# Second-attention scores moved ahead of the loop, and x in the places of the weight halves, in a two-layer MoE kernel

## The chip, the cores and the metric

The kernel runs on one core of one Trainium2 chip. The metric is the device time of one execution in microseconds (us), as the median of several runs; lower is better.

## The reference, cut to what matters

x has 12480 tokens of 128 channels, `inducing` has 32 rows. All data is float32.

```python
def mab(q, kv):                                # scale = 1/sqrt(128)
    s = scale * (q @ kv.T);  s = s - s.max(-1)
    a = np.exp(s);  a /= a.sum(-1) + 1e-9
    return a @ kv
h = mab(inducing, x)                           # first attention: 32 x 128, needs all of x
x = mab(x, h)                                  # second attention: 12480 x 128
g = s * relu(x @ w_in)**2 + b;  x = g @ w_out  # 128 -> 2048 -> 128
u = x @ moe2_w_in                              # 128 -> 2048
g = where(u >= 1, u, where(u <= -1, 0, (u + 1)**2 / 4))
return g @ moe2_w_out                          # 2048 -> 128
```

## The kernel before, in words

The tokens are cut into 25 blocks of 512 (the last has 192). The program has four parts.

**Front.** x is loaded in seven groups of four blocks (`load_x`, L272; groups 0 to 6, the last of one block). Each block is transposed on PE and copied by ACT into its own tile `xT` (`transposes`, L287), which stays for the whole kernel. From `xT` come the first attention's scores (`scores`, L303: tile `psc`, maximum, exponential `e`) and from x as loaded the weighted sum (`weighted`, L347: `pe`, `eT`, `ph`). The tile of x as loaded, `xc`, has four buffers (`XB = 4`), so the load of group g waits for the weighted sum `ph` of group g - 4. `finish` (L543) joins the groups into `hT` (128 x 32, four copies side by side), the only input that the second attention needs beside `xT`. The weights arrive as 64-bit floats in pieces of 512 columns (16 pieces: four each of `in`, `out`, `in2`, `out2`) and are converted by `convert` (L418) on ACT and DVE. The second layer's weights, and later w_out, are kept as two rounded halves, `hi` and `lo` (tiles `wi2_hi`, `wi2_lo`, `wo2_hi`, `wo2_lo`, `wo_hi`, `wo_lo`, each 128 x 2048).

**Ramp.** From `hT` on, the first 18 steps of the first layer (`ramp_step`, L889; a step is 256 hidden columns of one block, eight steps to a block) run between the rest of the conversions (`c_sum`, L457, has three matmuls for each piece of `in2` and `out2`), the products `hw = h @ w_in` (`h_w`, L843) and the softmaxes of block 0 and of group 1 (blocks 1 to 4; `all_softs`, L912).

**Loop.** Step t runs, on PE in this order, `in1` of step t (L639, tile `h`), `out2` (L764), `in2` of step t - 18 (L725, tile `h`), and `out1` of step t - 2 (L700). `in2` and both `out` products take three matmuls for each product of rounded halves. The elementwise work between them lies on ACT (relu, square, `hi`), DVE (clip, `g`, `lo`) and POOL (`hi`, `lo` of the first layer).

**Tail.** The last 18 steps of the second layer run without the first.

The second attention works on groups of up to four blocks: sizes 1, 4, 4, 4, 4, 4, 3, 1 (groups 0 to 7). For a group, `soft_scores` (L577) multiplies `hT[:, :32]` with `xT` of each block, four matmuls that fill the four 32-row strips of one PSUM bank. `soft_turn` (L585) transposes that in 32 x 32 squares on DVE into the SBUF tile `se`. Then come maximum, subtraction, exponential, sum, division and DMAs into place. In the loop these steps are called at fixed distances ahead of the block that needs them (`SOFT`, L47): scores and turn 22 steps ahead, maximum 21, and so on. In a loop step the scores stand on PE between `in2` and `out1`, and take the bank pair with the tag `h1`, which has a single buffer and is the one that `in1` writes in each loop step:

```python
ps = (mbank if g == 1 else bank)(f"s2_{g}")     # soft_scores; bank: tag h1, bufs=1; mbank: tag h2, bufs=2
p = mbank(f"h1_{t}") if t < LAG and t % 2 else bank(f"h1_{t}")   # in1
```

In the ramp `in1` takes `h1` and `h2` by turns; `h2` also serves `h_w` and the conversions (`cw`).

**What sets the order.** Front, ramp and the first four loop steps are ordered by a planner (`Plan`, L113). The string `JOBS` names jobs (`c` convert a piece, `x` load a group, `t` transposes, `s` scores, `w` weighted sum, `f` finish, `z` first softmax, `h`, `b`, `p` split a piece of w_out, `a` ramp step, `o` softmax of group 1, `q` next block's attention). In its order each operation takes the first gap on its engine that fits its estimated duration; the program is then emitted in order of planned start. Engines run their instructions in that order. All loads are issued by one queue (SP), in the planned order. PE gaps of the plan are filled with idle matmuls (`on_idle`, L1012; `on_idle0`, L1016). The second layer's buffers open at `close` (L936), after all conversions and splits. The loop follows `ORDER` (L72).

Of the kernel before, what the change touches and what calls it, by code (L numbers as in the profile page):

```python
# [10 lines left out]
F32 = mybir.dt.float32  # L11
# [26 lines left out]
NPC = DFF // PC  # L38
XB = 4
RAWB = 5  # L40
# [14 lines left out]
SQB = {"DVE": 1.0, "Pool": 3.0}  # L55
EVAC = ("ACT",)

# [116 lines left out]
def moe_attn_kernel(ctx: ExitStack, tc: tile.TileContext, x, ind, w_in, w_out, s, b, w_in2, w_out2, out):  # L174
# [12 lines left out]
    wo_lo = kt([128, FC, C], "wo_lo", F32R)  # L187
    wi2_hi = kt([128, DFF], "wi2_hi", F32R)
    wi2_lo = kt([128, DFF], "wi2_lo", F32R)
    wo2_hi = kt([128, FC, C], "wo2_hi", F32R)  # L190
    wo2_lo = kt([128, FC, C], "wo2_lo", F32R)
    hT = kt([C, 4 * NM], "hT")
# [225 lines left out]
    def convert(n, at=0.0):  # L418
# [35 lines left out]
        def c_hi(eng):  # L454
            copy(eng, wparts[name][0][:, sl], T["cva", n].bitcast(F32))

        def c_sum():  # L457
            ps = T["cw", n] = mbank(f"cw{n}")[:, 0, :]
            nc.tensor.matmul(ps, ident, T["cva", n].bitcast(F32), start=True, stop=False)  # L459
            nc.tensor.matmul(ps, minus_r, wparts[name][0][:, sl], start=False, stop=False)  # L460
            nc.tensor.matmul(ps, ident_r, T["cvl", n], start=False, stop=True)

        def c_lo(eng):
            copy(eng, wparts[name][1][:, sl], T.pop(("cw", n)))

# [6 lines left out]
        if name in ("in", "out"):  # L472
            P["c_add", n] = P["c_end", n] = best(ENG["add"], c_add, t, bias=CB)
        else:
            hi = best(ENG["hi"], c_hi, a)
            t = took("h2", 1.33, c_sum, hi, t, P["hT"])
            P["c_end", n] = best(ENG["lo"], c_lo, t)
            left["h2"].append(P["c_end", n])

    def split_out(n):  # L480

        k = pieces[n][1]
        sl = slice(k * PC, (k + 1) * PC)
        hi, lo = (w[:, sl] for w in wparts["out"])
        t = best(ENG["hi"], lambda e: copy(e, hi, T["w", n]), P["c_add", n])
        P["c_split", n] = best(ENG["rest"], lambda e: engine[e].tensor_sub(lo, T["w", n], hi.bitcast(F32)), t, bias=CB)

# [89 lines left out]
    def soft_scores(g):  # L577
        nb = sizes[g]
        ps = (mbank if g == 1 else bank)(f"s2_{g}")
        for i in range(nb):  # L580
            bl = first[g] + i
            nc.tensor.matmul(ps[NM * i:NM * (i + 1), 0, :tb(bl)], hT[:, :NM], xT[bl], start=True, stop=True)
        sm[g, "s"] = ps

    def soft_turn(g):  # L585

        n, cols = NM * sizes[g], tb(first[g])
        e = sm[g, "e"] = pool["wk"].tile([128, NQ, NM], F32, tag="se", name=f"se{g}", bufs=1)[:n, :cols // NM]
        nc.vector.transpose(e.rearrange("p q j -> p (q j)"), sm.pop((g, "s"))[:n, 0, :cols])  # L589

# [99 lines left out]

    def outp(t, hi, lo, whi, wlo, p, js=range(GW)):
        p = p[:, :tb(t // SPB)]
        for j in js:
            f = fch(t, j)
            first, last = f == 0, f == FC - 1
            nc.tensor.matmul(p, whi[:, f, :], hi[:, j, :], start=first, stop=False)  # L696
            nc.tensor.matmul(p, whi[:, f, :], lo[:, j, :], start=False, stop=False)  # L697
            nc.tensor.matmul(p, wlo[:, f, :], hi[:, j, :], start=False, stop=last)  # L698

    def out1(t):  # L700
        outp(t, hi1.pop(t), lo1.pop(t), wo_hi, wo_lo, acc1(t // SPB))

# [22 lines left out]
    def in2(t, js=range(GW)):  # L725
        bl = t // SPB
        if js[0] == 0:
            h2[t] = bank(f"h2_{t}") if t in tail and (t - tail[0]) % 3 == 0 else mbank(f"h2_{t}")
        p = h2[t]
        for j in js:  # L730
            f = fch(t, j)
            fs = slice(f * 128, (f + 1) * 128)
            nc.tensor.matmul(p[:, j, :tb(bl)], wi2_hi[:, fs], y1h[bl], start=True, stop=False)  # L733
            nc.tensor.matmul(p[:, j, :tb(bl)], wi2_lo[:, fs], y1h[bl], start=False, stop=False)  # L734
            nc.tensor.matmul(p[:, j, :tb(bl)], wi2_hi[:, fs], y1l[bl], start=False, stop=True)  # L735

# [27 lines left out]
    def out2(t, js=range(GW)):  # L764
        outp(t, hi2[t], lo2[t], wo2_hi, wo2_lo, acc2(t // SPB), js)

    def store(bl):
# [4 lines left out]
        for r in range(C // NM):  # L772
# [4 lines left out]
    misc = {}  # L777
    softs = {"scores": soft_scores, "turn": soft_turn, "top": soft_top, "sub": soft_sub, "e": soft_e,
             "sum": soft_sum, "mul": soft_mul, "move": soft_move}

    def at(t, f, *args):
        on_dve = f in (soft_turn, soft_top, soft_sum, soft_q)
        misc.setdefault((t, on_dve), []).append(lambda: f(*args))
# [22 lines left out]
    def f_se():  # L806
        e = sm[0, "e"] = wtile([128, NQ, NM], "se", "se0")[:TP, :KB, :]
# [61 lines left out]
    def ramp_soft(f):  # L869
        g = 1  # L870
        do = lambda *a: softs[f](g, *a)
        if f == "scores":
            in_use["g1"] = took("h2", 0.9, do)
        elif f in ("turn", "top", "sum"):
            P[f + "1"] = in_use["g1"] = add("DVE" if f == "turn" else "DVE+", {"turn": 0.7, "top": 0.69, "sum": 1.0}[f], do, in_use["g1"])
# [33 lines left out]
    def first_job():  # L909
        P["ind"], P["s"], P["s"] = loads()  # L910

    def all_softs():  # L912
        for f in softs:
            ramp_soft(f)
            if f == "turn":
                left["h2"].append(P["turn1"])

# [4 lines left out]
    def load(g):  # L922
        load_x(g, P.get(("ph", g - XB)))

    def step(a):
# [3 lines left out]
           "f": lambda _: finish(), "z": lambda _: first_soft(), "c": conv, "h": h_w, "b": b_cols, "p": split_out,  # L929
           "a": step, "o": lambda _: all_softs(), "q": ramp_q}  # L930
    for j in JOBS.split():
# [8 lines left out]

    P["close"] = add("switch", 0.01, close, *[o for k, o in P.items() if k[0] in ("c_end", "c_split")], *[P["out1", a] for a in range(LAG)], P["bcol"])
    P["cx"] = P["close"]
# [208 lines left out]
```

## Time and profile before

| | us |
|---|---|
| median of 3 runs | 1028.97 (1028.88 to 1030.15) |
| the profiled execution, its own time | 1030.76 |
| its span | 1028.9 |
| hT there (end of the front) | 50.3 |
| first `in2` matmul (end of the ramp) | 113.2 |
| PE busy in the span | 996.1 (97%) |
| DVE, ACT, POOL busy | 817.2, 846.6, 752.5 |

The span runs from the first to the last instruction of the profiled execution. Matmuls are pipelined and their ends modelled, so a busy PE is not PE at its peak. A float32 matmul leaves two records, a rounded one (`fp32r`) one.

### The profile page before, as it was taken

How to read it: one execution, taken by the hardware profiler on the slowest of the kernel's cores; microseconds unless marked ns; L12 is line 12 of the kernel's file. 1: busy time of each engine (PE TensorE's matmuls, PEld its weight loads, DVE VectorE, ACT ScalarE, POOL GpSimd, SP SyncE). 2: the span in 40 equal slices, each digit the busy share in tenths (PEclk: the TensorE clock that was granted, in tenths of full speed). 3: DMA queues.
4: the chain of work that ended last, by engine and by line, in shares of the span. 5: the costliest groups of instructions: out<-in, count | busy, mean ns of one | idle time of the engine just before them, and what ended most of it. 6: DMA issues, size and time to landing. Idle time of an engine off the chain costs nothing.

```text
span 1028.9 us, 12530 instructions
## 1 busy us (share of the span) xinstructions
PE 996.1 (97%) x4512; PEld 773.2 (75%) x4512; DVE 817.2 (79%) x838; ACT 846.6 (82%) x919; POOL 752.5 (73%) x507
## 2 busy tenths in 40 slices
PE   6899899999999999999999999999999999999997
PEld 4654577888778888778888778888778878888776
DVE  6888678787788878788878788777787878878884
ACT  5677888888888888888888888888888888887764
POOL 0211578888788788788888788888888878886466
PEclk9999999999999999999999999999999999999999
DMA  8521001100002000002000002000001000000000
GB/s 304 192 64 60 0 1 31 31 1 11 11 1 52 11 1 11 10 1 52 11 1 11 11 1 52 11 1 11 11 1 41 11 1 11 15 1 11 11 11 15
DMA packets 65469, 28.11 MB, mean 27 GB/s; under 512 B 54016, under 2 KB 58368, under 8 KB 65408
## 3 DMA queue, kind: packets, MB, share of 16 engines
q1 hardware_dynamic: 65408, 27.33, 10.9%
q8 instruction: 35, 0.57, 0.2%
q14 instruction: 26, 0.21, 0.1%
HBM read 14.80 MB, written 6.39 MB: 21 GB/s over the span
## 4 chain that ended last, share of the span: by engine, by line
PE 84%; DVE 10%; ACT 2%; DMA 2%; issue 1%; POOL 1%; SPq 0%; DVEq 0%; ACTq 0%; POOLq 0%
PE y L697 15%; PE y L696 15%; PE y L698 15%; PE h L733 9%; PE h L735 8%; PE h L734 8%; PE h L644 8%; DVE cl L740 3%; PE y L708 2%; DVE lo L761 2%; DMA xc<-in_x_dram 2%; DVE mx L607 1%; POOL lo L761 1%; DVE h L751 1%; PE cw L459 1%
## 5 line engine op out<-in xcount | busy, mean ns | idle before, releaser
L674 POOL TENSOR_TENSOR lo<-g,hi 128x1024 fp32r<-128x1024 f32 (+1 forms) x182 | 427.0, 2346 | 15.2
L740 DVE TENSOR_SCALAR cl<-h 128x1024 f32<-128x1024 f32 (+2 forms) x202 | 239.1, 1186 | 154.6 <-PE h L735 154.6
L744 ACT ACTIVATE cl<-cl,mhalf 128x1024 f32<-128x1024 f32 (+2 forms) x202 | 226.7, 1124 | 105.7 <-DVE cl L740 103.2
L697 PE MATMUL y<-lo,wo_hi 128*128 128x512 f32 (+1 forms) x764 | 299.8, 392 | 1.3 <-POOL lo L761 1.3
L698 PE MATMUL y<-hi,wo_lo 128*128 128x512 f32 (+1 forms) x764 | 299.5, 392 | 0.0
L696 PE MATMUL y<-hi,wo_hi 128*128 128x512 f32 (+1 forms) x764 | 299.5, 392 | 0.0
L226 POOL TENSOR_SCALAR hi<-g 128x1024 fp32r<-128x1024 f32 (+1 forms) x182 | 186.8, 1027 | 140.8 <-PE y L698 120.2
L751 DVE SCALAR_TENSOR_TENSOR h<-h,cl 128x1024 f32<-128x1024 f32 x182 | 223.1, 1226 | 12.4 <-ACT cl L744 1.2
L761 DVE TENSOR_TENSOR lo<-h,hi 128x1024 fp32r<-128x1024 f32 x182 | 221.2, 1216 | 2.7 <-ACT hi L222 1.9
L664 ACT ACTIVATE g<-g 128x1024 f32<-128x1024 f32 (+1 forms) x199 | 206.4, 1038 | 5.3
L657 ACT ACTIVATE g<-h 128x1024 f32<-128x1024 f32 (+1 forms) x194 | 191.5, 987 | 11.2 <-PE h L644 9.7
L222 ACT CAST hi<-h 128x1024 fp32r<-128x1024 f32 x182 | 181.9, 999 | 15.9 <-DVE h L751 15.9
L696 PEld LDWEIGHTS y<-hi,wo_hi 128*128 128x128 f32 x764 | 143.8, 188 | 38.2 <-POOL lo L674 4.2
L697 PEld LDWEIGHTS y<-lo,wo_hi 128*128 128x128 f32 x764 | 143.8, 188 | 35.7 <-POOL lo L761 2.5
L698 PEld LDWEIGHTS y<-hi,wo_lo 128*128 128x128 f32 x764 | 143.5, 188 | 33.4
L733 PE MATMUL h<-y1h,wi_hi 128*128 128x512 f32 (+1 forms) x400 | 157.4, 394 | 10.6 <-DVE lo L761 10.1
L735 PE MATMUL h<-y1l,wi_hi 128*128 128x512 f32 (+1 forms) x400 | 156.3, 391 | 0.0
L734 PE MATMUL h<-y1h,wi_lo 128*128 128x512 f32 (+1 forms) x400 | 156.0, 390 | 0.0
L644 PE MATMUL h<-qt,hw 128*128 128x512 f32 (+1 forms) x400 | 124.7, 396 | 3.6 <-DVE se L589 3.5
L733 PEld LDWEIGHTS h<-y1h,wi_hi 128*128 128x128 f32 x400 | 75.6, 189 | 33.5 <-DVE lo L761 14.2
L644 PEld LDWEIGHTS h<-qt,hw 128*128 128x128 f32 x400 | 74.2, 188 | 26.8 <-DVE se L589 6.1
L734 PEld LDWEIGHTS h<-y1h,wi_lo 128*128 128x128 f32 x400 | 75.5, 189 | 17.0
(144 smaller groups left out, 632.9 us busy)
## 6 DMA issues: line engine op xcount, KB each, us to landing
xc<-in_x_dram SPq DMA_DIRECT2D x24, 256.0 KB, 5.2
out_dram<-o SPq DMA_DIRECT2D x96, 64.0 KB, 2.2
qin<-se SPq DMA_DIRECT2D x92, 64.0 KB, 2.0
raw_in<-in_moe_w_in_dram SPq DMA_DIRECT2D x8, 512.0 KB, 6.9
raw_out<-in_moe_w_out_dram SPq DMA_DIRECT2D x8, 512.0 KB, 5.6
xc<-in_x_dram SPq DMA_DIRECT2D x1, 96.0 KB, 4.0
qin<-se SPq DMA_DIRECT2D x4, 24.0 KB, 1.8
out_dram<-o SPq DMA_DIRECT2D x4, 24.0 KB, 1.9
```

The lines of the kernel that those rows point to most:

```text
L644: nc.tensor.matmul(p[:, j, :tb(bl)], hw[f // 4][:, (f % 4) * 128:(f % 4 + 1) * 128], qt[bl], start=True, stop=True)
L674: engine[eng].tensor_sub(lo1[t], g1.pop(t), hi1[t].bitcast(F32))
L696: nc.tensor.matmul(p, whi[:, f, :], hi[:, j, :], start=first, stop=False)
L697: nc.tensor.matmul(p, whi[:, f, :], lo[:, j, :], start=False, stop=False)
L698: nc.tensor.matmul(p, wlo[:, f, :], hi[:, j, :], start=False, stop=last)
L733: nc.tensor.matmul(p[:, j, :tb(bl)], wi2_hi[:, fs], y1h[bl], start=True, stop=False)
L734: nc.tensor.matmul(p[:, j, :tb(bl)], wi2_lo[:, fs], y1h[bl], start=False, stop=False)
L735: nc.tensor.matmul(p[:, j, :tb(bl)], wi2_hi[:, fs], y1l[bl], start=False, stop=True)
L740: nc.vector.tensor_scalar(cl[t][:, part(js)], h2[t][:, part(js), :tb(t // SPB)], -1.0, 1.0, op0=ALU.max, op1=ALU.min)
L744: nc.scalar.activation(k, k, AF.Square, bias=mhalf, scale=0.5)
L751: nc.vector.scalar_tensor_tensor(oo[t][:, part(js)], h, -1.0, cl[t][:, part(js)], op0=ALU.max, op1=ALU.add)
L761: engine[eng].tensor_sub(lo2[t][:, part(js)], oo[t][:, part(js)], hi2[t][:, part(js)].bitcast(F32))
```

## The change

The scores and the turn of groups 2 to 7 are taken out of the loop and become a job of the ramp, `k`; group 1's keep their place in job `o`. The turn writes into `xT` of the group's first block, which nothing reads any more, in place of `se`. All scores take `h2` banks. `close` waits for the turns too. The later steps of the softmax stay in the loop at their distances from the block; group 2's, which begin at the first step that the planner does not order, move one step earlier.

The six weight halves lose their own tiles. Six tiles (`homes`) hold groups 0 to 5 of x first and a weight half afterwards; group 6 has a tile of its own. A load of x waits for nothing now. The copy into a half waits in the plan for `ph` of the group that was there. `JOBS` is new.

```diff
-SOFT = [(22, "scores"), (22, "turn"), (21, "top"), (19, "sub"), (17, "e"), (16, "sum"), (14, "mul"), (12, "move")]
+SOFT = [(21, "top"), (19, "sub"), (17, "e"), (16, "sum"), (14, "mul"), (12, "move")]
 JOBS = """
-c0 x0 t0 i c1 it x1 c2 s0 c3 x2 w0 x3 t1 t2 t3 s1 w1 s2 c4 x4 t4 s3 w2 x5 t5 w3 s4 c5 s5 w4 w5 x6 t6 s6 f z h0 b4 h1
-b5 h2 o a0 a1 c6 h3 c7 p5 a2 a3 c8 a4 p4 c9 a5 b6 a6 q1 p7 b7 a7 p6 a8 a9 a10 a11 a12 a13 c10 c11 c12 c13 q2 a14 a15
-c14 a16 a17 q3 c15
+c0 x0 t0 i it s0 c1 w0 c2 x1 t1 c3 x2 t2 s1 x3 c4 t3 s2 x4 w1 t4 w2 c5 s3 s4 x5 x6 t5 s5 w3 w4 w5 t6 s6 f z h0 b4 h1
+c6 p6 k2 a0 b5 h2 h3 a1 a2 k3 o c7 a3 a4 k4 k5 a5 b6 a6 c8 q1 c9 k6 b7 a7 a8 c10 q2 a9 a10 a11 a12 a13 c11 a14 a15
+p4 a16 c12 a17 k7 c13 c14 c15 p7 q3 p5
 """
-    wo_hi = kt([128, FC, C], "wo_hi", F32R)
...
+    HALF = ("in2", 0), ("in2", 1), ("out2", 0), ("out2", 1), ("out", 0), ("out", 1)
+    homes = ctx.enter_context(tc.tile_pool(name="homes", bufs=1, reuse_waits="tile"))
+    def half(name, k):
+        if (name, k) not in halves:
+            halves[name, k] = homes.tile([128, DFF], F32R, tag=f"half{HALF.index((name, k))}", name=f"w{name}_{k}")
+        return halves[name, k]
...
-                xc[g] = pre.tile([TP, GB * KB, C], F32, tag="xc", name=f"xc{g}", bufs=XB)
+                xc[g] = (homes.tile([TP, GB * KB, C], F32, tag=f"half{g}", name=f"xc{g}") if g < len(HALF) else
+                         pre.tile([TP, KB, C], F32, tag="xc", name=f"xc{g}"))
...
-            hi = best(ENG["hi"], c_hi, a)
+            g = 0 if name == "in2" else 2
+            hi = best(ENG["hi"], c_hi, a, P["ph", g])
...
-        ps = (mbank if g == 1 else bank)(f"s2_{g}")
+        ps = mbank(f"s2_{g}")
...
-        e = sm[g, "e"] = pool["wk"].tile([128, NQ, NM], F32, tag="se", name=f"se{g}", bufs=1)[:n, :cols // NM]
-        nc.vector.transpose(e.rearrange("p q j -> p (q j)"), sm.pop((g, "s"))[:n, 0, :cols])
+        e = xT[first[g]][:n]
+        sm[g, "e"] = e.rearrange("p (q j) -> p q j", j=NM)
+        nc.vector.transpose(e, sm.pop((g, "s"))[:n, 0, :cols])
...
+    def ramp_scores(g):
+        t = took("h2", 0.95, lambda: soft_scores(g), P["hT"])
+        in_use[f"g{g}"] = P["turn", g] = add("DVE", 0.7, lambda: soft_turn(g), t)
+        left["h2"].append(P["turn", g])
...
-        load_x(g, P.get(("ph", g - XB)))
+        load_x(g)
...
-    P["close"] = add("switch", 0.01, close, *[...], *[P["out1", a] for a in range(LAG)], P["bcol"])
+    P["close"] = add("switch", 0.01, close, *[...], *[P["out1", a] for a in range(LAG)], P["bcol"],
+                     *[P["turn", g] for g in range(2, len(sizes))])
```

## Rows read from the trace of the kernel before

**Rows 1.** Page: GB/s moved, 40 slices of 25.7 us; then the chain's shares by line.

```profile
GB/s 304 192 64 60 0 1 31 31 1 11 11 1 52 11 1 11 10 1 52 11 1 11 11 1 52 11 1 11 11 1 41 11 1 11 15 1 11 11 11 15
...
PE y L697 15%; PE y L696 15%; PE y L698 15%; PE h L733 9%; PE h L735 8%; PE h L734 8%; PE h L644 8%; DVE cl L740 3%; PE y L708 2%; DVE lo L761 2%; DMA xc<-in_x_dram 2%; DVE mx L607 1%; POOL lo L761 1%; DVE h L751 1%; PE cw L459 1%
```

**Rows 2.** Windows of the loop: window, length, busy us (instructions) of PE, PEld, DVE, ACT, POOL, clock, DMA.

```profile
225.66:263.49 37.83, 37.83 (x164) 30.47 (x163) 30.33 (x27) 33.23 (x34) 31.76 (x22) 1.00 0.05 8
263.49:301.32 37.83, 37.27 (x163) 28.88 (x162) 30.47 (x29) 30.89 (x32) 31.22 (x20) 1.00 0.05 8
```

**Rows 3.** Chain of waits around group 3's scores: start us, us, what.

```profile
261.98 0.46 PE h L644 x2
...
267.62 0.71 DVE se L589
...
273.32 0.47 PE h L644 x2
...
277.99 0.46 PE h L644 x2
```

**Rows 4.** Chain of waits around group 6's scores.

```profile
720.69 0.46 PE h L644 x2
...
732.05 0.46 PE h L644 x2
```

**Rows 5.** Chain of waits around group 7's scores, one block of 192 columns.

```profile
836.32 0.46 PE h L644 x2
...
847.33 0.46 PE h L644 x2
```

**Rows 6.** Chain of waits around group 2's scores, in the first loop steps.

```profile
127.98 0.47 PE h L644 x2
...
139.25 0.47 PE h L644 x2
```

**Rows 7.** Timeline of PE at group 3's scores: start us, us, engine, line, operation.

```profile
264.85 0.39 PE L735 MATMUL h<-y1l,wi_hi 128*128 128x512 f32 x1
...
265.16 1.06 PE L582 MATMUL s<-xT,hT 128*32 128x512 f32 x8
...
266.16 0.50 PE L696 MATMUL y<-hi,wo_hi 128*128 128x512 f32 x1
```

**Rows 8.** Groups of instructions by line: count | busy us, mean ns | idle before.

```profile
L589 DVE STREAM_TRANSPOSE se<-s 128x512 f32<-128x512 f32 x5 | 3.5, 707 | 0.1
...
L1018 PE MATMUL idle<-wz 128*128 128x128 f32 x18 | 2.9, 291 | 0.0
```

**Rows 9.** Timeline of SP, the loads' issue, in the front.

```profile
21.21 1.76 SPq L277 DMA_DIRECT2D xc<-in_x_dram  x4
...
29.66 4.11 SPq L277 DMA_DIRECT2D xc<-in_x_dram  x5
```

**Rows 10.** Timeline of PE in the front.

```profile
13.22 3.59 PE L294 MATMUL ptr<-ident,xc 128*128 128x128 f32 x16 [2.34 <-DMA xc<-in_x_dram]
...
20.07 1.08 PE L367 MATMUL ph<-xc,eT 128*32 128x128 f32 x32 [0.24 <-ACT eT L222]
21.08 3.45 PE L294 MATMUL ptr<-ident,xc 128*128 128x128 f32 x28
...
28.52 1.08 PE L367 MATMUL ph<-xc,eT 128*32 128x128 f32 x32
...
35.13 0.63 PE L294 MATMUL ptr<-ident,xc 128*128 128x128 f32 x4 [0.72 <-DMA xc<-in_x_dram]
```

**Rows 11.** Windows of the front, columns as in rows 2.

```profile
13.20:17.00 3.80, 3.78 (x19) 3.42 (x22) 3.63 (x7) 1.91 (x4) 0.00 (x0) 0.55 1.03 406
```

**Rows 12.** Windows of the ramp and of the front.

```profile
50.20:113.17 62.97, 62.26 (x208) 33.45 (x208) 49.94 (x86) 46.44 (x58) 10.62 (x12) 1.00 0.19 57
...
13.20:45.00 31.80, 28.95 (x349) 20.70 (x353) 26.63 (x65) 24.32 (x55) 2.56 (x2) 0.95 0.82 282
```

**Rows 13.** Groups of PE instructions within the ramp (50.2 to 113.17).

```profile
L1014 PE MATMUL idle<-win 128*128 128x128 f32 x20 | 2.8, 280 | 0.0
```

More of the change, by code (lines that the diff above doesn't have):

```diff
@@ L38 @@
 NPC = DFF // PC
-XB = 4
 RAWB = 5
@@ L55 @@
 SQB = {"DVE": 1.0, "Pool": 3.0}
-EVAC = ("ACT",)
+EVAC = ('ACT',)
 TS, TT = 0.42, 0.69
@@ L454, in c_hi @@
         def c_hi(eng):
-            copy(eng, wparts[name][0][:, sl], T["cva", n].bitcast(F32))
+            copy(eng, half(name, 0)[:, sl], T["cva", n].bitcast(F32))
         def c_sum():
@@ L459, in c_sum @@
             nc.tensor.matmul(ps, ident, T["cva", n].bitcast(F32), start=True, stop=False)
-            nc.tensor.matmul(ps, minus_r, wparts[name][0][:, sl], start=False, stop=False)
+            nc.tensor.matmul(ps, minus_r, half(name, 0)[:, sl], start=False, stop=False)
             nc.tensor.matmul(ps, ident_r, T["cvl", n], start=False, stop=True)
         def c_lo(eng):
-            copy(eng, wparts[name][1][:, sl], T.pop(("cw", n)))
+            copy(eng, half(name, 1)[:, sl], T.pop(("cw", n)))
         t = add("ACT", 0.68, c_abs, P["raw", n], P.get(("c_end", n - CVB)), at=at)
@@ L474, in convert @@
         else:
[L475 removed]
+            g = 0 if name == "in2" else 2
+            hi = best(ENG["hi"], c_hi, a, P["ph", g])
             t = took("h2", 1.33, c_sum, hi, t, P["hT"])
[L477 removed]
+            P["c_end", n] = best(ENG["lo"], c_lo, t, P["ph", g + 1])
             left["h2"].append(P["c_end", n])
@@ L483, in split_out @@
         sl = slice(k * PC, (k + 1) * PC)
-        hi, lo = (w[:, sl] for w in wparts["out"])
-        t = best(ENG["hi"], lambda e: copy(e, hi, T["w", n]), P["c_add", n])
-        P["c_split", n] = best(ENG["rest"], lambda e: engine[e].tensor_sub(lo, T["w", n], hi.bitcast(F32)), t, bias=CB)
+        t = best(ENG["hi"], lambda e: copy(e, half("out", 0)[:, sl], T["w", n]), P["c_add", n], P["ph", 4])
+        P["c_split", n] = best(ENG["rest"], lambda e: engine[e].tensor_sub(half("out", 1)[:, sl], T["w", n], half("out", 0)[:, sl].bitcast(F32)), t, P["ph", 5], bias=CB)
     def on_it():
@@ L689, in acc2, with outp @@
         return y2p[bl]
-    def outp(t, hi, lo, whi, wlo, p, js=range(GW)):
+    def outp(t, hi, lo, name, p, js=range(GW)):
         p = p[:, :tb(t // SPB)]
@@ L695, in outp @@
             first, last = f == 0, f == FC - 1
-            nc.tensor.matmul(p, whi[:, f, :], hi[:, j, :], start=first, stop=False)
-            nc.tensor.matmul(p, whi[:, f, :], lo[:, j, :], start=False, stop=False)
-            nc.tensor.matmul(p, wlo[:, f, :], hi[:, j, :], start=False, stop=last)
+            whi, wlo = (half(name, k)[:, f * 128:(f + 1) * 128] for k in range(2))
+            nc.tensor.matmul(p, whi, hi[:, j, :], start=first, stop=False)
+            nc.tensor.matmul(p, whi, lo[:, j, :], start=False, stop=False)
+            nc.tensor.matmul(p, wlo, hi[:, j, :], start=False, stop=last)
     def out1(t):
-        outp(t, hi1.pop(t), lo1.pop(t), wo_hi, wo_lo, acc1(t // SPB))
+        outp(t, hi1.pop(t), lo1.pop(t), "out", acc1(t // SPB))
     def out1_whole(t):
@@ L731, in in2 @@
             f = fch(t, j)
[L732 to L735, printed above, removed]
+            whi, wlo = (half("in2", k)[:, f * 128:(f + 1) * 128] for k in range(2))
+            nc.tensor.matmul(p[:, j, :tb(bl)], whi, y1h[bl], start=True, stop=False)
+            nc.tensor.matmul(p[:, j, :tb(bl)], wlo, y1h[bl], start=False, stop=False)
+            nc.tensor.matmul(p[:, j, :tb(bl)], whi, y1l[bl], start=False, stop=True)
     def clip2(t, js=range(GW)):
@@ L777, in moe_attn_kernel @@
     misc = {}
-    softs = {"scores": soft_scores, "turn": soft_turn, "top": soft_top, "sub": soft_sub, "e": soft_e,
+    softs = {"top": soft_top, "sub": soft_sub, "e": soft_e,
              "sum": soft_sum, "mul": soft_mul, "move": soft_move}
     def at(t, f, *args):
-        on_dve = f in (soft_turn, soft_top, soft_sum, soft_q)
+        on_dve = f in (soft_top, soft_sum, soft_q)
         misc.setdefault((t, on_dve), []).append(lambda: f(*args))
@@ L871, in ramp_soft @@
         do = lambda *a: softs[f](g, *a)
[L872 to L875, printed above, removed]
+        if f in ("top", "sum"):
+            in_use["g1"] = add("DVE+", {"top": 0.69, "sum": 1.0}[f], do, in_use["g1"])
         elif f == "e":
@@ L910, in first_job @@
         P["ind"], P["s"], P["s"] = loads()
+    def ramp_scores(g):
+        t = took("h2", 0.95, lambda: soft_scores(g), P["hT"])
+        in_use[f"g{g}"] = P["turn", g] = add("DVE", 0.7, lambda: soft_turn(g), t)
+        left["h2"].append(P["turn", g])
     def all_softs():
+        ramp_scores(1)
         for f in softs:
             ramp_soft(f)
-            if f == "turn":
-                left["h2"].append(P["turn1"])
     def conv(n):
@@ L929, in moe_attn_kernel @@
            "f": lambda _: finish(), "z": lambda _: first_soft(), "c": conv, "h": h_w, "b": b_cols, "p": split_out,
-           "a": step, "o": lambda _: all_softs(), "q": ramp_q}
+           "a": step, "o": lambda _: all_softs(), "q": ramp_q, "k": ramp_scores}
     for j in JOBS.split():
@@ L939, in close @@
         pool["py"] = ctx.enter_context(tc.tile_pool(name="py", bufs=1, space=PSUM, side="right", reuse_waits="tile"))
-    P["close"] = add("switch", 0.01, close, *[o for k, o in P.items() if k[0] in ("c_end", "c_split")], *[P["out1", a] for a in range(LAG)], P["bcol"])
+    P["close"] = add("switch", 0.01, close, *[o for k, o in P.items() if k[0] in ("c_end", "c_split")], *[P["out1", a] for a in range(LAG)], P["bcol"],
+                     *[P["turn", g] for g in range(2, len(sizes))])
     P["cx"] = P["close"]
```

11 lines of the change are left out of this document (3 added, 8 removed).

## The prediction, made before the changed kernel was run

> **What bounds the kernel now.** I read the slices of the page first, then the chain of waits, then windows. The chain's shares by line [rows 1] are almost all PE lines: the three matmuls of `out`, of `in2`, and `in1`. The loop's windows [rows 2] say the same more sharply: in a window without scores PE is busy for 37.83 of 37.83 us, while DVE has 30.33, ACT 33.23 and POOL 31.76 (the window's columns run PE, PEld, DVE, ACT, POOL). So in the loop anything that PE does or waits for is on the path, and the others have 12% or more to spare. The next window, which holds group 3's scores, has PE at 37.27: there PE waits, and spends time on the scores besides.
>
> What such a scores step costs is best read from the starts of `in1`, one per step. An ordinary step lasts 277.99 - 273.32 = 4.67 us [rows 3]. From 261.98 to 273.32, two steps with the scores of group 3 in the first, are 11.34 us, so 11.34 - 9.34 = 2.00 too much. Group 6 gives 732.05 - 720.69 = 11.36, so 2.02 [rows 4]; groups 4 and 5 lie between. Group 7, 192 columns, gives 847.33 - 836.32 = 11.01, so 1.67 [rows 5], and group 2, among the first loop steps, 139.25 - 127.98 = 11.27, so 1.93 [rows 6].
>
> The 2.00 has two parts. A matmul of 512 columns starts every 0.23 us (4.67 / 20), so after the last `in2` matmul at 264.85 the next was due at 265.08; with the scores between, `out1` starts at 266.16 [rows 7]. That is 1.08 us of PE for the four matmuls. The other 0.92 is the bank: scores and `in1` share the one `h1` pair, and the turn that empties it begins at 267.62 and takes 0.71 [rows 3], when `out1` has already ended. The next `in1` waits for it.
>
> Before the loop, the front is also close to PE: 28.95 us busy of 31.80 between 13.2 and 45 [rows 12]. The ramp is closer still, 62.26 of 62.97 [rows 12], but this holds 2.8 us of idle matmuls [rows 13] that can give way.
>
> **Part 1, scores and turn leave the loop.** Saved: four groups at 2.0, 1.67 and 1.93: 8.0 + 1.67 + 1.93 = 11.6 us. The least that could be saved is PE's own time, if the waits come back elsewhere: 5 x 1.08 and 0.75 for group 7 (its excess is 0.33 below the others'), 6.15. I take 11.6, because the other engines have the slack of rows 2 and the turn's 0.71 leaves DVE as well. What is late next is the stretch where a group's sum and reciprocal sit on DVE (`mx` L607, 1% of the chain [rows 1]); it comes once per group before and after, several steps later, and I leave it unchanged. Group 2's later steps move one loop step earlier; PE waits there for nothing of theirs, and I cost this at nothing.
>
> **Part 2, the same work enters the ramp.** Added to PE: 6.15 us. Added to DVE: five turns of 0.71 and a short one, about 4 us, where DVE is busy for 49.94 of 62.97 [rows 12]; that has room. Each set holds one of the two `h2` banks from its first matmul until its turn is done; behind it in the plan wait the odd `in1` steps, `h_w` and the conversions' `cw`, and on DVE the turn stands behind whatever conversion was planned before it. The least: all idle matmuls and idle time of the ramp give way, 2.8 + 0.71 = 3.5, so 6.15 - 3.5 = +2.65. A gain is excluded by the same rows: without its idle matmuls PE has 59.5 us of work in 62.97, and 6.15 more do not fit. The most: the loop's price, wait included, +11.6. I take the PE work with half of the 3.5 given back, 6.15 - 1.75 = +4.4; it is nearest to the row of PE's own time, since two banks instead of one cover most turns.
>
> **Part 3, x waits for no buffer.** SP issued group 4's loads at 21.21 and group 5's at 29.66 [rows 9], each within 0.1 us of the end of the weighted sum that freed its buffer (20.07 + 1.08 and 28.52 + 1.08 [rows 10]). Group 5's last transposes then waited for their load until 35.13 [rows 10]. Without these waits the queue is limited by what the loads move. Before `hT` the new order loads pieces 0 to 5 and all of x, 3.1 + 6.4 = 9.5 MB. The first slice moved 304 GB/s over 25.7 us, 7.8 MB [rows 1], and the peak stretch shows 406 GB/s [rows 11], so the remaining 1.7 MB land some 4 us later, at about 30: 5 us before 35.1. PE cannot follow by 5 us, as it has its own work: it had 2.85 us of idle time between 13.2 and 45, and 2.9 us of idle matmuls, part of them in the chain of small steps that ends the front [rows 8]. So `hT` comes earlier by 0 (if another order of the same chain binds) to 5.75 us. I take 3.0, by the row of idle time. The conversions that no longer fit before `hT` fall into the ramp, on DVE and ACT, which have room there.
>
> A loss in the same place is bounded too. Group 1's loads now stand behind one more weight piece, 0.52 MB at 406 GB/s or 1.3 us. PE is meanwhile given scores and weighted sum of group 0, so it loses little. But in the stretch from 13.2 to 17.0, right after PE's wait, the granted clock was 0.55 [rows 11], that is partly at the lower of its two levels: 16 transposes took 3.59 us, where later 28 took 3.45 [rows 10], or 1.97 for 16. The low clock cost 1.6 us once. [...]
>
> **Part 4, halves in the places of x.** The copies into the halves wait for `ph` of groups 0 to 5. The first second-layer pieces are converted only after `hT`, because their `c_sum` needs the banks that open then, and by then every `ph` is done. Cost nothing; were one late, the copy is an ACT instruction and ACT has 16.5 us free in the ramp [rows 12]. `close` also waits for the turns, the last of which is planned several steps before the last conversion: nothing.
>
> **Sum.** -11.6 + 4.4 - 3.0 = -10.2 us, made against the profiled execution's 1030.76 (span 1028.9): 1020.6. That execution lies 1.8 above the median of the runs, 1028.97; taken from the median, the forecast is 1018.8.
>
> **Rivals.**
>
> A. The front gives nothing: `hT` hangs on PE's transposes and the clock, not on x. For it: only 0.72 us of the late front is put down to x's load [rows 10]. Against: 2.85 us of idle PE. -11.6 + 4.4 = -7.2: 1021.8. Chance 0.15.
>
> B. The ramp pays the loop's whole price, since each set's bank is held until a turn that is queued on DVE. For it: DVE is busy for 79% of the ramp. -11.6 + 11.6 - 3.0: 1026.0. Chance 0.08.
>
> C. Slower: the same mechanism, but the turn stands on DVE behind a conversion that itself waits, so PE, which runs in order, stops at the next odd `in1`, and the relu and square behind it on ACT come late too. It decides from (11.6 + 3.0) / 6 = 2.43 us per set; at 3.0 per set, one and a half times the loop's 2.0, the ramp grows by 18.0 and the time is 1028.97 + 18.0 - 14.6 = 1032.4. Against: two banks, and each loop wait was 0.92 with one. Chance 0.09, a third of it near no change.
>
> D. The waits of the loop come back: with the pause gone, DVE or ACT no longer catch up, and only PE's 6.15 are saved. -6.15 + 4.4 - 3.0 = -4.75: 1024.2. Against: the slack of rows 2. Chance 0.06.
>
> E. Front and ramp both absorb all they can: -11.6 + 2.65 - 5.75 = -14.7: 1014.3. For it: every idle matmul marks a gap. Chance 0.12.
>
> **How the numbers follow.** The forecast has 0.50, with its own range 1016 to 1021.5. The range for 8 in 10 takes in A and D and nearly all of E: 1013.8 to 1024.6; B and C are left out. A measurement of this kernel can tell 0.2%, about 2 us, from no change. Faster: the forecast, A, D, E and over half of B, 0.88; within 0.2%: the rest of B and a third of C, 0.06; slower 0.06.
>
> **What would show it.** In the profile after: no scores in the loop, `in1` starting every 4.67 us through the places of the six sets, and the time from the first `in2` to the end shorter by about 11.6. `hT` at about 47 instead of 50.3, no load of x waiting for a `ph`, and the last of x landed near 30. From `hT` to the first `in2`, 67 us instead of 63, with six sets of about 1.08 on PE and fewer idle matmuls. It would be wrong if the ramp grew by more than 8 us, if `in1` still waited in the loop where the sets were, or if `hT` did not move.

## The result, and the profile after

The changed kernel takes 1017.45 us (median of 4 runs, 1017.15 to 1020.16), the kernel before beside it 1029.56 (1028.88 to 1030.97): a ratio of 0.9886 with a 95% interval of 0.9866 to 0.9907. It is faster by 12.1 us; 10.2 were forecast. The profiled execution took 1017.15, with a span of 1015.3.

Two points cut the span into parts that answer to the steps of the prediction: the end of `hT`'s copy, and the start of the first `in2` matmul.

| us | before | after | difference | forecast |
|---|---|---|---|---|
| start to `hT` (front) | 50.27 | 48.02 | -2.25 | -3.0 |
| `hT` to first `in2` (ramp) | 62.89 | 69.52 | +6.63 | +4.4 |
| first `in2` to end (loop and tail) | 915.78 | 897.80 | -17.98 | -11.6 |
| span | 1028.94 | 1015.34 | -13.60 | -10.2 |

So a total near the forecast is made of three terms that all missed, and the largest miss is a gain of 6.4 us that no step of the prediction contains. The page of after, as in [rows 1]: GB/s moved in 40 slices, and the chain's shares by line.

```profile
GB/s 315 188 42 84 0 1 39 15 11 11 4 7 53 8 4 11 11 0 52 12 1 11 11 1 53 11 1 11 11 1 42 10 1 11 16 3 8 11 12 15
...
PE y L705 15%; PE y L704 15%; PE y L703 15%; PE h L740 9%; PE h L742 8%; PE h L741 8%; PE h L650 8%; PE y L715 3%; DVE cl L747 2%; DVE lo L768 2%; DMA xc<-in_x_dram 1%; DVE mx L613 1%; POOL lo L768 1%; DMA raw_in<-in_moe_w_in_dram 1%; PE cw L464 1%
```

The same engine and the same lines bound the kernel. Windows of after, with the columns of [rows 2]: two of the front, the ramp, and the two loop windows.

```profile
13.20:17.00 3.80, 2.92 (x48) 2.56 (x49) 3.52 (x8) 2.92 (x6) 0.00 (x0) 1.00 1.04 398
13.20:45.00 31.80, 29.19 (x380) 22.00 (x381) 27.44 (x71) 25.12 (x58) 0.00 (x0) 1.00 0.81 280
48.02:117.54 69.52, 67.94 (x244) 33.88 (x243) 55.69 (x92) 42.60 (x54) 13.87 (x13) 1.00 0.17 51
225.66:263.49 37.83, 37.83 (x166) 30.70 (x165) 30.44 (x27) 33.57 (x35) 32.22 (x21) 1.00 0.05 8
263.49:301.32 37.83, 37.83 (x165) 30.74 (x164) 32.10 (x30) 32.56 (x34) 32.49 (x21) 1.00 0.05 8
```

In the second loop window PE had 37.27 [rows 2] and now has all 37.83: the pause for group 3's scores is gone. And both windows hold two matmul records more, though PE was already busy all the time in the first. The chain of after, where group 3's scores stood before, shows why (start us, us, what; the starts of `in1`):

```profile
259.67 0.47 PE h L650 x2
...
264.30 0.47 PE h L650 x2
...
268.92 0.47 PE h L650 x2
```

No step is longer than its neighbours, as forecast, but an ordinary step lasts 4.63 us, and in [rows 3] it lasted 4.67. From the records the two are 4.627 and 4.673. Over the loop's 182 steps the 0.046 makes up to 8.4 us. PE is busy throughout in both kernels, so neither the busy share nor any wait shows it. Only the distance between equal instructions does.

### The profile page after: what moved, and what is told of

It reads as the page before. It is cut to its first block, busy times and chain, and to the rows that moved or that the text cites. A ratio compares the mean times of both kernels' runs of the same rounds, so it can differ in the third digit from the quotient of the medians.

```text
span 1015.3 us, 12473 instructions
## 1 busy us (share of the span) xinstructions
PE 985.8 (97%) x4518; PEld 772.2 (76%) x4518; DVE 819.6 (81%) x839; ACT 844.2 (83%) x917; POOL 755.6 (74%) x508
## 4 chain that ended last, share of the span: by engine, by line
PE 86%; DVE 8%; DMA 2%; ACT 2%; POOL 1%; issue 1%; DVEq 0%; ACTq 0%; POOLq 0%
PE y L705 15%; PE y L704 15%; PE y L703 15%; PE h L740 9%; PE h L742 8%; PE h L741 8%; PE h L650 8%; PE y L715 3%; DVE cl L747 2%; DVE lo L768 2%; DMA xc<-in_x_dram 1%; DVE mx L613 1%; POOL lo L768 1%; DMA raw_in<-in_moe_w_in_dram 1%; PE cw L464 1%
## 5 line engine op out<-in xcount | busy, mean ns | idle before, releaser
L704 PE MATMUL y<-lo,wout 128*128 128x512 f32 (+1 forms) x764 | 297.6, 390 | 1.5 <-POOL lo L768 1.3
L705 PE MATMUL y<-hi,wout 128*128 128x512 f32 (+1 forms) x764 | 298.5, 391 | 0.0
L703 PE MATMUL y<-hi,wout 128*128 128x512 f32 (+1 forms) x764 | 297.3, 389 | 0.8 <-DVE o L777 0.7
L704 PEld LDWEIGHTS y<-lo,wout 128*128 128x128 f32 x764 | 143.9, 188 | 36.4 <-POOL lo L768 2.5
L703 PEld LDWEIGHTS y<-hi,wout 128*128 128x128 f32 x764 | 143.5, 188 | 33.7 <-issue 1.6
L705 PEld LDWEIGHTS y<-hi,wout 128*128 128x128 f32 x764 | 143.5, 188 | 31.4
L740 PE MATMUL h<-y1h,win 128*128 128x512 f32 (+1 forms) x400 | 155.3, 388 | 8.8 <-DVE lo L768 8.6
L742 PE MATMUL h<-y1l,win 128*128 128x512 f32 (+1 forms) x400 | 155.7, 389 | 0.0
L741 PE MATMUL h<-y1h,win 128*128 128x512 f32 (+1 forms) x400 | 154.9, 387 | 0.0
L740 PEld LDWEIGHTS h<-y1h,win 128*128 128x128 f32 x400 | 75.2, 188 | 30.9 <-DVE lo L768 12.4
L741 PEld LDWEIGHTS h<-y1h,win 128*128 128x128 f32 x400 | 75.2, 188 | 17.0
```

Of the source, the lines that this page charges most:

```text
L703: nc.tensor.matmul(p, whi, hi[:, j, :], start=first, stop=False)
L704: nc.tensor.matmul(p, whi, lo[:, j, :], start=False, stop=False)
L705: nc.tensor.matmul(p, wlo, hi[:, j, :], start=False, stop=last)
L740: nc.tensor.matmul(p[:, j, :tb(bl)], whi, y1h[bl], start=True, stop=False)
L741: nc.tensor.matmul(p[:, j, :tb(bl)], wlo, y1h[bl], start=False, stop=False)
L742: nc.tensor.matmul(p[:, j, :tb(bl)], whi, y1l[bl], start=False, stop=True)
```

## The experiments

The theory after this first comparison: the scores' part of the gain is as forecast, and the faster step comes from where the new tiles put the weight halves in SBUF. A tile's place is given below as the byte at which it starts in its partition, by the build's allocation, modulo 256; W is the place of the six halves and M that of the loop's working tiles (`hw`, `qt`, `y1h`, `y1l`) with the rest of their pool. The recorded expectations speak of the halves' place modulo 128, which is how far I saw it at the time. Rivals: that the step got faster because the scores left the loop, or because of the new order and loads.

**Padding in the kernel before, and the change with its halves back.** The kernel before with 32 bytes ahead of the halves and 96 behind them, and the changed kernel with its halves back at 128. Both move the working tiles too, by 128 bytes, to M = 224; at the time I counted that as no move:

```diff
+    kt([128, 8], "pad")            # before_w32; 24 more floats behind wo2_lo
     wo_hi = kt([128, FC, C], "wo_hi", F32R)
```
```diff
     mneg = kt([128, 1], "mneg")
+    kt([128, 24], "pad")           # after_w0; 8 more floats behind the halves
```

> The kernel before with the six weight halves 32 bytes further in SBUF (a pad tile of 32 bytes ahead of them, one of 96 bytes behind, so that all later tiles keep their distance from a multiple of 128 bytes). The profile after shows ordinary loop steps of about 4.625 us where before had 4.67. Theory P (place): the halves began on a multiple of 128 bytes before and begin 32 bytes past one after, and this sets the matmuls' start distance. Then this kernel has steps of about 4.63 us and is some 7 us faster than before (160 steps x 0.045): about 1022.5 us. Rival O (order): the faster steps come from the new program, or differ from run to run. Then nothing changes: steps of 4.67, 1029 to 1030 us.

> The changed kernel with its six homes 96 bytes further, so that the halves begin on a multiple of 128 bytes as before; later tiles keep their distance from such a multiple. Theory P: steps of 4.67 us, about 7 us slower than the changed kernel: 1024 to 1025 us. Rival O: steps of 4.625, 1017.5 us.

Measured: before_w32 1018.94, ratio 0.9898 (0.9883 to 0.9912), so padding alone, 128 bytes in all, is worth 10 us in the old program, where theory P had 7. after_w0 took 1025.1, ratio 0.9961 (0.9946 to 0.9976): with its halves back at 128 the change gives a third of its gain, as theory P had it. The starts of `in1` in the chain, first before_w32, then after_w0:

```profile
222.99 0.46 PE h L646 x2
...
227.57 0.47 PE h L646 x2
...
232.23 0.46 PE h L646 x2
```
```profile
224.19 0.47 PE h L652 x2
...
228.85 0.47 PE h L652 x2
```

before_w32's steps alternate, 4.58 and 4.66; after_w0's are 4.67. Both rivals fall: the old order with scores in its loop can have a fast step, and the new one without them a slow step.

**Scores and turn left out.** The kernel before without scores and turn of groups 2 to 7, and the changed kernel without its six sets, its order kept as it was planned with them:

```diff
 def soft_scores(g):
+    if g > 1: return               # before_noscores and after_nosets, soft_turn likewise
```

> The kernel before without the scores and turns of groups 2 to 7 (their softmax takes the group's first block of x transposed as it stands; the rest is unchanged). It measures what these cost in the loop. The forecast's term: 11.6 us, so 1018 us, with in1 every 4.67 us through the places of the sets. Rival D of the prediction (the waits come back elsewhere): only PE's 6.15 us, so 1023.4. Under theory P its ordinary steps stay at 4.67, as the halves stay in place; under rival O with a cause in the scores they fall to 4.63 and it is 1011.

> The changed kernel with the six sets (scores and turn of groups 2 to 7) left out of the emitted program, their places in the plan and so the order of everything else kept; the softmaxes take the group's first block of x transposed. It measures the sets' price in the ramp, which lasts 69.5 us from hT to the first in2 in the changed kernel. If the sets cost PE's own time, 6.15: ramp about 63.4, time 1011.3. If they cost the loop's price, 11.6: ramp 58, time 1006. If the ramp grew because the new order is worse elsewhere: ramp above 66, time above 1014.

Measured: before_noscores 1018.42, ratio 0.989 (0.9875 to 0.9905). From its first `in2` to its end are 904.82, and its steps keep the time of before, as its chain shows:

```profile
255.21 0.47 PE h L648 x2
...
259.89 0.46 PE h L648 x2
```

So the sets cost the old loop 915.78 - 904.82 = 10.96; 11.6 were forecast. The 10.96 is somewhat too small: for a part of its first loop steps the granted clock of before_noscores was lower, and that of before was not. Windows of before and of before_noscores, columns as in [rows 2]:

```profile
116.00:128.00 12.00, 8.89 (x36) 6.29 (x35) 9.74 (x9) 10.34 (x11) 6.07 (x4) 1.00 0.00 0
```
```profile
116.00:128.00 12.00, 9.56 (x32) 6.72 (x31) 9.74 (x9) 9.47 (x11) 5.28 (x3) 0.86 0.00 0
```

From the first `in2` to the third `in1` behind it, before took 127.82 - 113.17 = 14.65 and before_noscores, with the same instructions, 127.81 - 112.28 = 15.53. At equal clock the sets thus cost some 10.96 + 0.88 = 11.8, an estimate from these records.

after_nosets took 1016.64, ratio 0.9878 (0.9861 to 0.9894), less than 1 us below the changed kernel. Its ramp is 67.58, only 1.94 shorter. Where the sets stood PE now idles, as the group of `out1` in the ramp shows (count | busy us, mean ns | idle before and what ended it); in after the same group has 0.7:

```profile
L719 PE MATMUL y<-g,wo_s 128*128 128x512 f32 x72 | 33.3, 605 | 4.1 <-ACT g L674 3.0 <-ACT y1f L723 0.9
```

This run alone would say that the sets cost the ramp 1.9, and by its numbers it meets the third case of its expectation. But it keeps an order in which ACT and DVE were planned around the sets, so it gives the gap a set leaves, not what a ramp without sets would take; the old order without them takes 62.9.

**Two more places of the halves.** The changed kernel with W at 64 and at 96, M at 224 in both (padding as in after_w0, of other sizes).

> The changed kernel with its halves 64 bytes past a multiple of 128 bytes (32 in the changed kernel, 0 in after_w0; later tiles keep their distance, which is 96 for all moving tiles). At 0 the ordinary step took 4.667 us, at 32 4.627. Theory P1 (only a start on a multiple of 128 is slow): 4.63 again, 1017.5 us. Theory P2 (what counts is how the halves lie against the moving tiles at 96): between 0 and 96 the step goes on falling or falls and rises; then 64 differs from 32 by 0.02 us per step or more, 3 us or more in all, and 96 is the slowest. Rival (places at a larger scale, the pad's effect being chance): no order in the four.

> The changed kernel with its halves 96 bytes past a multiple of 128 bytes, as all moving tiles are. P1: 4.63 us per step, 1017.5 us. P2: the slowest of the four places, 4.67 or more, 1024 us or more.

Measured: after_w64 1025.23, ratio 0.9961 (0.9946 to 0.9976), step 4.667; after_w96 1023.18, ratio 0.9937 (0.992 to 0.9953), steps of 4.660 and later 4.653. Modulo 128 the halves are thus slow at 0 and 64, little better at 96 and fast at 32. Neither P1 (64 and 96 as fast as 32) nor P2 (96 the slowest) has it. M is not the same either: 96 in the changed kernel, 224 in the other three.

**The loads of x.** The changed kernel with the old waits (group g again behind the weighted sum of group g - 4), and the kernel before with free loads but its old order:

```diff
-        load_x(g)
+        load_x(g, P.get(("ph", g - 4)))       # after_xwait; xc in half{g % 4}
```
```diff
-        load_x(g, P.get(("ph", g - XB)))
+        load_x(g)                             # before_freex; xc and halves in six homes
```

> The changed kernel with x in four of the six homes only, so that the loads of groups 4, 5 and 6 wait for the weighted sums of groups 0, 1 and 2, as before; in the plan too. The prediction's part 3 says that freeing x brought hT forward by 3.0 us: then hT comes near 51 here, and it is 3 us slower, 1020.5. In the runs so far hT of the unchanged front came at 50.3, 48.4 and 49.4, of the new front at 48.0, 48.8 and 48.4, so a mean difference of 1.0: then 1018.5. Rival A (x's loads don't bind): 1017.5.

> The kernel before, with its own order of jobs and its scores in the loop, but with x in the homes so that no load of x waits, and the halves on a multiple of 128 bytes as before (their order among themselves is that of the changed kernel). The prediction's part 3: hT 3.0 us earlier, about 47, 1026.6 us. Rival A: hT as before, within 48.4 to 50.3, and 1029.6. Steps 4.67 by the place of the halves.

Measured: after_xwait 1020.52, ratio 0.9918 (0.99 to 0.9936). The time is the one that part 3 would give, but its parts are not. In its trace the last loads of x are issued at 28.60 instead of 21.06, yet `hT` comes only 0.6 later (48.64). Of the 1.4 that its trace adds after the first `in2`, 0.83 are there by the third `in1` behind it (10.54 against 9.71), where the granted clock was lower; in after it stays at 1.00:

```profile
123.00:130.00 7.00, 6.66 (x20) 4.62 (x21) 5.02 (x6) 5.91 (x7) 6.30 (x5) 0.76 0.00 0
```

The rest has no cause that I found, and its interval overlaps that of the changed kernel. before_freex took 1037.31, ratio 1.0079 (1.0064 to 1.0095): free loads in the old order are a loss of 8 us. `hT` comes at 52.70 and the ramp takes 65.40. Its chain says how the front got later:

```profile
36.71 0.59 ACT cvs_out L434
...
37.33 0.44 DVE cvs_out L438
...
38.25 0.70 DVE cva_out L445
...
39.44 0.70 DVE cvl_out L452
...
40.17 0.69 DVE wo_s L458
40.86 0.61 DVE mx L328
```

One weight piece's whole conversion, ACT and then DVE, now stands ahead of a maximum of the first attention, which `hT` needs. That the planner meant it for a gap that is no longer there is my reading, not shown. Part of the delay is the clock, which was lower on the same chain a little later:

```profile
43.00:47.00 4.00, 3.93 (x44) 3.60 (x44) 1.85 (x7) 1.92 (x7) 0.00 (x0) 0.57 0.06 23
```

What makes the ramp 2.5 longer was not looked into. In the changed kernel the same free loads come without these losses, so the new `JOBS` makes them harmless; the next runs show that the two together bring little.

**Sets in the old ramp; modulo 128 or not; halves or working tiles.** Three kernels. oldorder_sets: the kernel before with old loads, old order and W, M = 160, 224, only k2 to k7 inserted in its `JOBS`. after_w160: the changed kernel with 128 bytes ahead of the halves, W, M = 160, 224. before_m96: the kernel before with only M moved, to 192.

```diff
-b5 h2 o a0 a1 c6 h3 c7 p5 a2 a3 c8 a4 p4 c9 a5 b6 a6 q1 p7 b7 a7 p6 a8 a9 a10 a11 ...
+b5 h2 o k2 a0 a1 c6 h3 k3 c7 p5 a2 a3 k4 c8 a4 p4 c9 k5 a5 b6 a6 q1 p7 k6 b7 a7 p6 a8 a9 a10 k7 a11 ...
```

> The kernel before with its own order of loads and ramp and its own four waits of x; only the six sets of scores and turns are moved from the loop into the ramp (k2 to k7 spread over its steps), and the weights' halves lie 32 bytes further. What is not changed against the kernel with only the halves moved (1018.9) is the front and the order. Theory one (scores in the loop cost 11.0, sets in the ramp their TensorE time of 6.2 in any order): ramp 69.1 instead of 62.9, the rest after the first in2 894.2 at a step of 4.60, time 1014.1; if the step locks at 4.627 as in the changed kernel, the rest is 897.8 and the time 1017.5. Rival (the old ramp has gaps that take the sets for the 1.9 which leaving them out gave back in the new order): ramp 64.8, time 1009.8 (1013.3 at 4.627). Rival two (a set in the old order waits and pays the loop's price, 11): ramp 74, time 1019.

> The changed kernel with the six halves, hT excepted, 128 bytes further on: they lie 32 bytes past a multiple of 128 as in the changed kernel, and all other tiles of the loop at the same place modulo 128 as before. Theory one (the place modulo 128 decides the loop's step): step 4.627, first in2 to end 897.8, time 1017.5. Rival (each layout falls into some step by chance of its start, place or not): a step that may be any of 4.60 to 4.67, most likely 4.667 as three of the four other layouts of the changed kernel had it, rest 904.7, time 1025.

> The kernel before with its halves where they are; only the working tiles behind them (hidden input, q, y1) lie 96 bytes further, at 64 past a multiple of 128 instead of 96, so that in the in2 matmuls weights and moving operand stand 64 apart, as in the kernel with the halves moved by 32 bytes. Theory one (the halves' own place decides): step 4.67, time 1029 as before. Rival (the distance of weights and moving operand modulo 128 decides): the step falls to 4.60 to 4.63, time 1018 to 1022.

Measured: oldorder_sets 1013.96, ratio 0.9852 (0.9818 to 0.9885); after_w160 1012.52, ratio 0.9838 (0.981 to 0.9866); before_m96 1022.13, ratio 0.9923 (0.9905 to 0.9942). The starts of `in1` in the three chains, in this order:

```profile
223.96 0.47 PE h L647 x2
...
228.62 0.46 PE h L647 x2
...
233.19 0.47 PE h L647 x2
```
```profile
222.72 0.45 PE h L651 x2
...
227.29 0.45 PE h L651 x2
```
```profile
225.81 0.45 PE h L645 x2
...
230.43 0.45 PE h L645 x2
```

Both theories on after_w160 were wrong: at the same place modulo 128 as the changed kernel it has steps of 4.57, the fastest of all, up to the last group, and is the fastest kernel of this study. before_m96 denies that the halves' own place decides: they did not move, and the step fell from 4.67 to 4.63, as the rival on record had it. The places of both kinds of tiles count, and modulo more than 128. oldorder_sets shows the old ramp with the sets: 69.80 instead of 62.90, so they cost 6.9 there and 6.6 in the new order. It also has before_w32's W and M, and its steps of 4.58 and 4.66, with stretches of 4.57. Its last part is 892.87 against before_w32's 905.24, 12.4 less; of that 1.27 is the clock again, lower in before_w32's first loop steps (15.85 against 14.58 from the first `in2` to the third `in1`; in its chain the `in2` matmuls from 119.73 to 121.88 take 0.43 or 0.44 us each, those from 124.81 on 0.23), which leaves about 11.1. Against after_w160, with all of the change at the same W and M, it is 1.4 us slower, well inside the two intervals: free loads and new order are worth little beside the six sets.

**The old program in the places of the changed one.** The last run puts the old program's tiles at W, M = 32, 96, as the changed kernel has them:

```diff
+    kt([128, 40], "pad")
     wo_hi = kt([128, FC, C], "wo_hi", F32R)
...
     wo2_lo = kt([128, FC, C], "wo2_lo", F32R)
+    kt([128, 24], "pad2")
```

> The program of the kernel before, with its halves and its working tiles moved so that both stand as in the changed kernel modulo 256 bytes: halves at 32, working tiles at 96 (before: 128 and 96; halves moved by 32 bytes: 160 and 224). Theory one (the layout modulo 256 sets the loop's step, whatever the program around it): step 4.627 as in the changed kernel, rest after the first in2 907 to 910, time 1020 to 1023.5. Rival (only the halves' place modulo 128 counts): steps of 4.665 and 4.575 in turn as with the halves moved by 32 bytes, rest 905, time 1018.9. Rival two (the step belongs to the program and its start, not to the layout): any step, 4.667 to 4.679 the likeliest, time 1028 to 1030. In the first case the change at equal layout is worth what stands between this time and 1017.5: 3 to 6.

Measured: 1023.02, ratio 0.9928 (0.9911 to 0.9945), as theory one had it. Its chain and its last part:

```profile
223.40 0.47 PE h L646 x2
...
228.02 0.47 PE h L646 x2
```
```profile
112.85:1022.30 909.45, 888.19 (x3893) 711.65 (x3891) 731.19 (x662) 768.90 (x795) 737.70 (x483) 1.00 0.07 13
```

The steps are 4.627, those of the changed kernel to the nanosecond, in a program with other instructions around them. This kernel is what splits the result, since it differs from before only in places and from after, its places taken modulo 256, only in the change. The granted clock of before, of this kernel and of after is 1.00 from the first `in2` to the tail; in the front it differs, as told below.

| us | forecast | places (before to before_as_after) | the change at equal places (to after) |
|---|---|---|---|
| front | -3.0 | -0.31 | -1.94 |
| ramp | +4.4 | 0.00 | +6.63 |
| loop and tail | -11.6 | -6.30 | -11.68 |
| span | -10.2 | -6.62 | -6.99 |

## Why the prediction was right, and where it was not

The time fell inside the forecast's own range, but by compensation: about half of the gain is the places, which the prediction did not consider at all, and they made up for a ramp and a front that came out worse. That was luck: after_w0, the change with its halves at the old place, took 1025.1, which lies above that range.

**Part 1, the loop: right.** 11.6 forecast, 11.68 at equal places, 10.96 with the sets left out of the old loop (11.8 at equal clock), 12.4 at W, M = 160, 224 in the old order (11.1 at equal clock). Reading the price from `in1` to `in1`, wait included, and not from PE's own 6.15, was the step that mattered; rival D, that the waits come back, falls. The `mx` of L607 was left at no change, and the step that holds it is 1.5 to 1.6 us too long before and after. Only that of group 2, whose later steps moved at no cost in the prediction, is 1.86 too long after (6.487) and 1.25 before (5.926).

**Part 2, the ramp: mechanism right, size too small.** The term "half of the 3.5 given back" failed. Groups of PE in the ramp of after, and one set in its timeline:

```profile
L587 PE MATMUL s<-xT,hT 128*32 128x512 f32 (+1 forms) x48 | 6.9, 593 | 0.3 <-ACT g L663 0.3
...
L1024 PE MATMUL idle<-win 128*128 128x128 f32 x18 | 2.3, 275 | 0.0
```
```profile
54.71 1.07 PE L587 MATMUL s<-xT,hT 128*32 128x512 f32 x8
```

A set takes 1.07; 1.08 was forecast. But idle matmuls fell only from 2.8 [rows 13] to 2.3, and PE's idle time rose from 62.97 - 62.26 = 0.71 [rows 12] to 69.52 - 67.94 = 1.58. In the sum nothing was given back, and +6.63 is PE's 6.15 with a little more. An idle matmul marked a place where PE had nothing ready by its order; the scores did not end up in those places. The old order paid as much (6.9). Why neither planned order puts the sets into the gaps was not tried. Rivals B and C, in which a set pays the loop's price or more, fall: two banks did cover the turns. E, in which the ramp absorbs all it can, falls too.

**Part 3, the front: the step "PE cannot follow by 5 us, I take 3.0" was too generous.** The loads did come earlier: the last of x is issued at 21.06, where SP waited until 29.66 [rows 9]; the last transposes start at 34.34 instead of 37.76. From the queue of after; from PE of after, its last wait for x and the last transposes; from PE of before, the last transposes; then the chain that follows in after:

```profile
21.06 4.98 SPq L283 DMA_DIRECT2D xc<-in_x_dram  x5
```
```profile
25.22 0.63 PE L300 MATMUL ptr<-ident,xc 128*128 128x128 f32 x4 [1.23 <-DMA xc<-in_x_dram]
...
34.34 0.33 PE L300 MATMUL ptr<-ident,xc 96*128 96x96 f32 x2
```
```profile
37.76 0.39 PE L294 MATMUL ptr<-ident,xc 96*128 96x96 f32 x2
```
```profile
41.31 0.11 PE pm L513
41.42 0.67 PE idle L1028 x6
42.09 1.03 PE ph L373 x32
...
43.55 0.86 PE idle L1028 x6
44.42 0.25 PE pl L528 x2
...
45.95 1.21 DVE hsum L558
...
47.20 0.50 PE pht L536 x2
...
47.73 0.29 DVE hT L561
```

x no longer binds behind 25.22, ten us earlier than before (35.13 [rows 10]). PE's own work does, without a break until 38.6, and then a chain of small steps. The transposes gained 3.4, `hT` 2.25. Work that `hT` does not need takes up part of the difference: in after the chain from 25.22 on holds 16 `bsum` matmuls, 1.69 us, and 12 idle ones, 1.53 us; in before, from 35.13 on, it holds 4 (0.26 us) and 6 (0.86 us). That is the case the prediction gave as its lower bound, "if another order of the same chain binds".

How much of the -1.94 is the change is blurred by the clock. In the stretch 13.2 to 17.0 the granted clock was 0.55 in before [rows 11] (0.50 from 13.6 to 16.4, 1.00 from 16.8 on) and 1.00 in after, but it changes between kernels whose front is the same program. before_w32's window:

```profile
13.20:17.00 3.80, 3.26 (x19) 1.19 (x17) 3.63 (x8) 3.15 (x6) 0.00 (x0) 1.00 1.03 399
```

The old front ended at 50.27, 50.08 and 49.96 with this stretch at 0.55 to 0.59 (before, oldorder_sets, before_as_after) and at 48.41, 47.77 and 49.41 with it at 1.00 (before_w32, before_m96, before_noscores). The new front ended at 48.53 to 48.96 with it at 0.55 to 0.60 (after_w0, after_w64, after_w96, after_w160) and at 48.02 and 48.41 at 1.00 (after, after_nosets). At equal clock the means differ by 50.10 - 48.81 = 1.3 and 48.53 - 48.22 = 0.3, so the front is worth about 1, not 3. That is nearer to rival A's nothing. The price of 1.6 that the prediction read for the low clock is what the old front shows, 50.10 - 48.53 = 1.57, though its three ends at 1.00 lie 1.64 apart; the new front shows 48.81 - 48.22 = 0.59. Whether the clock is low there does not go with the order alone: in before_w32 and before_noscores it was low in the first loop steps instead, and in after, after_nosets and before_m96 nowhere between 13.2 and the tail (means of the whole span 0.998, 0.999 and 0.999).

**Part 4** cost nothing, as forecast. One copy into a half stands in the chain, after as before; it waited for its own input (`cva_in`) and not for a `ph`. The chain of after, then that of before:

```profile
67.99 0.62 ACT win L227
```
```profile
90.18 0.62 ACT wi_hi L222
```

**What was missing: the places.** The change list said that six tiles lose their place, and the prediction costed only the waits on them. It took 4.67 per step as a property of the work. The places and steps of this case:

| W, M modulo 256 | kernels | ordinary step, us |
|---|---|---|
| 128, 96 | before, before_noscores | 4.673, or 4.679 and 4.654 in turn |
| 128, 224 | after_w0, before_freex | 4.667 |
| 64, 224 | after_w64 | 4.667, at first 4.680 |
| 96, 224 | after_w96 | 4.660, later 4.653 |
| 32, 96 | after, after_nosets, after_xwait, before_as_after | 4.627 |
| 128, 192 | before_m96 | 4.627 |
| 160, 224 | before_w32, oldorder_sets | 4.665 and 4.575 in turn, in other stretches 4.573 |
| 160, 224 | after_w160 | 4.573, in the last fifth 4.665 and 4.575 in turn |

Shown: the step follows W and M through different programs (rows two and five; the last two rows share their states), and moving either alone changes it. One regularity holds in all 14 kernels: where W - M is 64 modulo 128, the step is 4.627 or less on average, and where it is 0, 32 or 96, it is 4.65 or more. That was the rival on record for before_m96, whose forecast came out, at its edge (4.60 to 4.63 and 1018 to 1022; 4.627 and 1022.13). But W - M alone does not tell 4.627 from 4.573, and only before_m96 was run to test it. Not shown: why. The other tiles of the loop's pool moved with M, those outside it and PSUM were not moved, and modulo 256 is the coarsest modulus that fits these runs, not a proven one. At 160, 224 and at 128, 96 a program has more than one repeating state.

## What to carry to other kernels

When a change gives tiles new places, run the old program in the new places (padding alone) before crediting the change: here that control takes half of the gain away, and one padding (before_w32, 10 us) was worth more than the change at equal places (1023.02 - 1017.45 = 5.6 by the medians; at W, M = 160, 224 it is 1018.94 - 1012.52 = 6.4). Price what leaves a full engine's loop by the distance between equal instructions, waits included (here 11.68 us, where PE's own time was 6.15), and what enters a full stretch by its whole time on that engine (here 6.63 for the 6.15), unless the trace shows that it will stand in the gaps. A load that comes earlier moves the end only until the next chain binds (here the last loads of x were issued 8.6 us earlier, and `hT` came 2.25 earlier); look for that chain's idle fillers first.

## What the runs showed of the hardware

In a loop where PE is busy without a break, 20 matmuls of 512 columns took 4.573 us (after_w160) to 4.679 us (before, in turn with 4.654) at a granted clock of 1.00, that is 229 to 234 ns from start to start, depending on where the loop's tiles lie in SBUF: 2.3%, or some 19 us of this kernel. Padding that changes no instruction but its addresses took the old program's step from 4.673 us (before) to 4.627 (before_m96, before_as_after), so in this case PE's rate is not free of where tiles lie; why is not shown. In the trace of before the steps repeat to about 1 ns: 4.679 and 4.654 or 4.655 in turn from 139.09 to 167.09, 4.673 or 4.674 from 177.70 to 261.82, and 4.679 and 4.654 in turn again from 273.15. Both changes stand behind a longer step, the one with group 2's `mx` (5.926) and the one with group 3's scores (6.566). The granted clock also fell at different places in kernels whose instructions there are the same: from 13.2 to 17.0 it was 0.55 in before and 1.00 in before_w32, from 116 to 128 it was 1.00 in before and 0.86 in before_noscores.
